# Six instead of fourteen whole-float32 products, k loaded by two heads, and a new written-out order of steps

## The chip, the cores and the metric

The kernel runs on one core of one Trainium2 chip. The metric is the device time of one execution in microseconds (us), the median of three runs. TensorE (PE in the profile) multiplies, VectorE (DVE) and ScalarE (ACT) do the elementwise work, GpSimd (POOL) and SyncE (SP) mostly start transfers (DMA). The engines run side by side, and each takes its own instructions strictly in the order in which the program lists them.

## The reference

Everything is float32. For 8 images with 8 heads, 576 positions and 64 features per head:

```python
q_s = softmax(q over features);  k_s = softmax(k over positions)
kv  = einsum('bhsd,bhse->bhde', k_s, v)          # 64 x 64 per head
x   = einsum('bhsd,bhde->bhse', q_s, kv)         # rows of 512
h   = x @ w_in                                   # 512 -> 2048
out = (h * cos(h)) @ w_out                       # 2048 -> 512
```

## The kernel before

Images 0, 1, 2 go through the two big products one after the other in *units*: unit (b, f) takes image b's 512 main rows and the f-th of 16 slices of 128 columns of `w_in`. Its first product (`unit1`) gives h in a PSUM bank, `gated` forms h·cos(h) with four instructions that alternate between ScalarE (`turns`, L1144), VectorE (`rest`, L1148), ScalarE (`cos`, L1154) and VectorE (`gate`, L1159), and the second product (`unit2`) multiplies by a slice of `w_out` into four accumulators. Units 0 to 7 are image 0 with f = 0 to 7, units 8 to 15 image 1 with f = 0 to 7; then come image 0 and image 1 with f = 8 to 15, and image 2. There are two banks for h, so the first product of unit u waits for the gate of unit u-2. Images 3 to 7 and the rows left over from all images follow as three pairs with a seven-product scheme (`block`, L1491).

A product in units is done in one of two ways. *Split*: each operand is held as a high part that TensorE's fast float32 form takes exactly, and a low rest; three of these matmuls replace one (L1119, L1204). Making the parts costs a copy on ScalarE (`hi`, `late_hi`) and a subtraction on VectorE (`lo`, `late_lo`) for each operand: for a slice of weights (`split` in `convert`), for x (`late`), for the gated h (`split_g`). *Whole*: the operands stay plain float32, and one matmul takes longer (L1111, L1197). `XP` is the number of units of image 0 whose first product is whole (8), `F2` the number of units whose second product is whole (6). For these the weights wait in a spare place (`room`) and their parts are made later. Weights need two ScalarE and two VectorE instructions (`bias`, `bits`, `shift`, `sign`) before any use.

Attention of each image (`k_exps`, `k_steps`, `q_steps`, `x_steps`) runs in between: q and k by two groups of four heads, maximum and exponent on VectorE, GpSimd and ScalarE, kv and x on TensorE. At the start TensorE also multiplies zeros (`fill`, `warm_up`).

`Plan` collects all this as numbered steps, each with an engine and an assumed duration: 0.69 us for a VectorE instruction on 128x512, 0.60 to 0.66 for one on ScalarE. The list `ORDER` holds the step numbers, and the program is emitted in that order; the list alone sets the order of each engine's instructions and of SP's transfers. An instruction waits for its operands by semaphore, and everything behind it on its engine waits too.

A load of k is a step of `load_k` on SP: one transfer of 512 KB (four heads) and one of 64 KB (left-over rows). The first v load (`load_v`, image 0, first group) is one of 512 KB and one of 64 KB; all other v loads are of two heads.

Of the kernel before, what the change touches and what calls it, by code (L numbers as in the profile page):

```python
# [27 lines left out]
    XP=8,  # L28
# [3 lines left out]
    F2=6,  # L32
# [15 lines left out]
    bus=dict(k=1.13, q=1.24, v=1.12, i=1.6, o=1.4),  # L48
# [323 lines left out]
def linear_attention_then_cos_gated_mlp(  # L372
# [247 lines left out]
    def load_k(b, a, place, due, eng="SP"):  # L620
# [9 lines left out]
        def load_main():  # L630
            t, q_of = T["k4", b, a], QUEUE[eng]
            q_of.dma_start(
                t[:, :, 0:CM, :], src[:, 0:NM, :].rearrange("h (p c) d -> p h c d", c=CM)
            )
# [5 lines left out]
        def load():  # L640
            load_main()
            load_left()
# [1111 lines left out]
```

## Time and profile before

| | |
|---|---|
| median of 3 runs | 860.26 us (857.47 to 862.21) |
| the profiled execution's own time | 860.02 us |
| its span, first to last instruction | 858.2 us |
| granted TensorE clock, mean | 0.995 of full speed |
| busy: TensorE, weight load, VectorE, ScalarE, GpSimd | 98%, 76%, 71%, 63%, 11% |
| HBM | 175 GB/s over the span |

Busy shares are of the whole span. The page also cuts the span into 40 slices and follows one chain of releases back from the last instruction; other views group instructions by line, list who waited for whom, or give the busy time of every engine in a chosen stretch. A matmul on whole float32 leaves two records and so counts twice there ("x8" for four matmuls).

### The profile page before, as it was taken

To read this page: it belongs to the slowest core of one execution; us is meant where nothing else is said; L and a number is where in the kernel's file an instruction comes from. 1 tells how busy PE (TensorE), PEld (TensorE's weight loads), DVE (VectorE), ACT (ScalarE), POOL (GpSimd) and SP (SyncE) were. 2 spreads that over 40 slices of the span, in tenths; PEclk is the share of its full clock that TensorE was granted. 3 is DMA by queue.
4 is the path that set the end of the run, shared out by engine and by line. 5 is a ranking of instruction groups with operands and counts; after the bars stand their busy time and mean duration, and the time that the engine had idled before them with its cause. 6 is when DMAs were issued, how large, how long until landed. Compare 5 with 4: busy or idle time off the path is not lost.

```text
span 858.2 us, 12494 instructions
## 1 busy us (share of the span) xinstructions
PE 838.4 (98%) x4292; PEld 656.1 (76%) x4292; DVE 609.0 (71%) x989; ACT 536.9 (63%) x1065; POOL 92.8 (11%) x149
## 2 busy tenths in 40 slices
PE   5999999999999999999999999999999999999997
PEld 5754788777777777777777888887788888888886
DVE  6798889988888878786776867855458646454543
ACT  5789899869678465765754855445446544453441
POOL 1100100110100101112112011111100211021000
PEclk9899999999999999999999999999999999999999
DMA  9972497634888895786776685665633736162213
GB/s 227 291 222 92 154 249 205 205 96 130 225 274 264 255 352 155 192 239 179 206 226 178 186 202 133 195 178 142 194 90 106 210 101 179 49 197 62 62 39 109
DMA packets 162495, 151.31 MB, mean 176 GB/s; under 512 B 66432, under 2 KB 128640, under 8 KB 162432
## 3 DMA queue, kind: packets, MB, share of 16 engines
q1 hardware_dynamic: 142080, 105.94, 42.7%
q0 software_dynamic: 19968, 44.05, 18.1%
q8 instruction: 34, 0.56, 0.3%
q10 hardware_dynamic: 384, 0.52, 0.2%
q14 instruction: 29, 0.24, 0.1%
HBM read 107.74 MB, written 42.73 MB: 175 GB/s over the span
## 4 chain that ended last, share of the span: by engine, by line
PE 75%; DMA 10%; SPq 5%; issue 5%; ACT 2%; DVE 2%; POOL 0%; DVEq 0%; ACTq 0%; POOLq 0%
PE acc L1204 35%; PE z L1491 13%; PE a L1491 10%; PE h L1119 7%; PE h L1111 3%; PE acc L1197 2%; DMA out_dram<-o 2%; PE x L966 2%; PE kv L813 2%; DMA k<-in_k_dram 1%; SPq L944 1%; DMA q_left<-qb 1%; DMA v<-in_v_dram 1%; SPq L666 1%; DMA s<-w_own 1%
## 5 line engine op out<-in xcount | busy, mean ns | idle before, releaser
L1491 PE MATMUL z<-xs,s 128*128 128x512 f32 x576 | 146.7, 391 | 1.0 <-DMA s<-w_sums 0.4
L1491 PEld LDWEIGHTS z<-xs,s 128*128 128x128 f32 x576 | 107.4, 188 | 26.3 <-issue 2.1
L1119 PE MATMUL h<-x,w_i 128*128 128x512 f32 x480 | 115.8, 392 | 1.5 <-DVE kt L1159 1.5
L1491 PE MATMUL a<-xs,s 128*128 128x512 f32 x432 | 109.9, 390 | 0.3 <-DVE kt_('s', 0, 1, 3)_3626 L1159 0.3
L1119 PEld LDWEIGHTS h<-x,w_i 128*128 128x128 f32 x480 | 89.2, 188 | 23.0 <-DVE kt L1159 2.8
L1204 PE MATMUL acc<-w_o,ghi 128*128 128x512 f32 x336 | 105.2, 394 | 1.0 <-DVE o L1246 0.9
L1491 PEld LDWEIGHTS a<-xs,s 128*128 128x128 f32 x432 | 80.9, 188 | 18.4 <-DVE glo_('s', 1, 2, 0)_5905 L1179 0.8
L1204 PEld LDWEIGHTS acc<-w_o,ghi 128*128 128x128 f32 x336 | 62.2, 188 | 18.2 <-issue 2.7
L1204 PE MATMUL acc<-w_o,glo 128*128 128x512 f32 x168 | 65.5, 390 | 0.0
L1512 DVE TENSOR_TENSOR c<-a,c 128x512 f32<-128x512 f32 x48 | 33.0, 688 | 35.6 <-PE a L1491 35.6
L1505 ACT COPY c<-z 128x512 f32<-128x512 f32 x48 | 28.1, 586 | 46.2 <-PE z L1491 38.2
L1465 POOL DMA_DIRECT2D s<-w_sums x48 | 30.2, 631 | 199.2 <-PE a L1491 130.9
L1465 POOL DMA_DIRECT2D s<-w_own x48 | 30.5, 636 | 195.0 <-PE z L1491 96.6
L1512 DVE TENSOR_TENSOR c<-z,c 128x512 f32<-128x512 f32 x24 | 16.6, 690 | 43.3 <-PE z L1491 32.7
L870 ACT ACTIVATE q<-q,qm 128x64 f32<-128x64 f32 x126 | 42.0, 337 | 1.8 <-DVE qm L857 1.8
L1144 ACT ACTIVATE kt<-h 128x512 int32<-128x512 f32 x48 | 28.5, 595 | 22.9 <-PE h L1119 20.2
L1148 DVE SCALAR_TENSOR_TENSOR kt<-kt,h 128x512 f32<-128x512 int32 x48 | 32.7, 680 | 10.7 <-ACT kt L1144 10.7
L762 POOL PARTITION_ALL_REDUCE m<-m x32 | 27.4, 901 | 110.1 <-DVE m L756 107.2
L1154 ACT ACTIVATE stash<-stash 128x512 f32<-128x512 f32 x48 | 30.1, 630 | 12.4 <-DVE stash L1148 12.4
L1204 PEld LDWEIGHTS acc<-w_o,glo 128*128 128x128 f32 x168 | 31.5, 188 | 6.7
L1154 ACT ACTIVATE kt<-kt 128x512 f32<-128x512 f32 x48 | 30.5, 635 | 9.8 <-DVE kt L1148 9.5
L1159 DVE TENSOR_TENSOR kt<-kt,h 128x512 f32<-128x512 f32 x42 | 28.4, 677 | 8.0 <-ACT kt L1154 8.0
(887 smaller groups left out, 1795.0 us busy)
## 6 DMA issues: line engine op xcount, KB each, us to landing
s<-w_sums POOLq DMA_DIRECT2D x48, 512.0 KB, 5.1
s<-w_own POOLq DMA_DIRECT2D x24, 512.0 KB, 4.8
q<-in_q_dram SPq DMA_DIRECT2D x32, 256.0 KB, 3.6
k<-in_k_dram SPq DMA_DIRECT2D x16, 512.0 KB, 5.2
raw_i<-in_moe_w_in_dram SPq DMA_DIRECT2D x16, 512.0 KB, 6.3
raw_o<-in_moe_w_out_dram SPq DMA_DIRECT2D x16, 512.0 KB, 6.2
v_sb<-in_v_dram SPq DMA_DIRECT2D x30, 256.0 KB, 4.7
q_rows<-qb SPq DMA_DIRECT2D x96, 64.0 KB, 2.7
```

The lines of the kernel that those rows point to most:

```text
L762: nc.gpsimd.partition_all_reduce(T["m", b, a][:, hs].rearrange("p h d -> p (h d)"), T["m1", b, a][:, hs].rearrange("p h d -> p (h d)"), P, ...
L870: nc.scalar.activation(t[:, r], t[:, r], AF.Exp, bias=m[:, r : r + 1], accum_out=o[:, r : r + 1])
L1119: nc.tensor.matmul(o, a, x, start=(c == 0 and n == 0), stop=(c == KC - 1 and n == 2))
L1144: nc.scalar.activation(t.bitcast(I32), src(), AF.Identity, bias=0.25, scale=1.0 / TWO_PI)
L1148: nc.vector.scalar_tensor_tensor(t, t.bitcast(I32), -TWO_PI, src(), op0=ALU.mult, op1=ALU.add)
L1154: nc.scalar.activation(t, t, AF.Sin, bias=0.5 * math.pi)
L1159: nc.vector.tensor_mul(o, t, src())
L1204: nc.tensor.matmul(T["acc", j], a[:, js], w, start=(first and n == 0), stop=(last and n == 2))
L1465: nc.gpsimd.dma_start(t, src)
L1491: nc.tensor.matmul(o, a, x, start=(first and c == 0 and m == 0), stop=(c == 1 and m == 2), skip_group_check=not first,)
L1505: "ACT", 0.6, lambda: nc.scalar.copy(cell(place), T["z" + to, k, n]),
L1512: lambda: nc.vector.tensor_add(cell(place), T["z" + to, k, n], cell(place)),
```

## The change

`XP` becomes 4 and `F2` 2: the first products of units 4 to 7 and the second products of units 2 to 5 are split. Their weights no longer wait in a room but pass at once through the two places `wc`; image 0's x is needed in parts from unit 4 on, and the gated h of units 2 to 5 is split too. The 512 KB transfer of k becomes two of 256 KB, by two heads each, in every load; the first load of v becomes two of 256 KB, by halves of its columns. `ORDER` is another list, 3050 numbers instead of 3036.

```diff
-    XP=8,
+    XP=4,
-    F2=6,
+    F2=2,
...
-        def load_main():
-            t, q_of = T["k4", b, a], QUEUE[eng]
+        def load_main(i):
+            t, q_of, hs = T["k4", b, a], QUEUE[eng], slice(2 * i, 2 * i + 2)
             q_of.dma_start(
-                t[:, :, 0:CM, :], src[:, 0:NM, :].rearrange("h (p c) d -> p h c d", c=CM)
+                t[:, hs, 0:CM, :], src[hs, 0:NM, :].rearrange("h (p c) d -> p h c d", c=CM)
             )
...
         def load():
-            load_main()
+            load_main(0)
+            load_main(1)
             load_left()
...
-            plan.load(CFG["bus"]["k"] * 2, load, writes=places, due=due, parts=2, eng=eng)
+            plan.load(CFG["bus"]["k"] * 2, load, writes=places, due=due, parts=3, eng=eng)
...
-        def get_main(src, main):
+        def get_main(src, main, x=slice(0, 2)):
+            n = main.shape[1] // 2
             QUEUE[eng].dma_start(
-                main[:, :, 1 : WV - 1],
-                src[:, 0:NM, :].rearrange("h (p x c) d -> p x h (c d)", x=2, c=2),
+                main[:, x.start * n : x.stop * n, 1 : WV - 1],
+                src[:, 0:NM, :].rearrange("h (p x c) d -> p x h (c d)", x=2, c=2)[:, x],
             )
...
-            plan.load(CFG["bus"]["v"] * 1.7, load_main, writes=place, due=due, eng=eng)
+            for x in range(2):
+                plan.load(CFG["bus"]["v"] * 0.85, lambda x=x: load_main(x), writes=[place[x]], due=due, eng=eng)
```

The two lists can be read against the steps. Up to the first product of unit 11 (image 1, f = 3; the last VectorE step that it needs is the gate of unit 9, for the bank) they hold:

| listed before it | old list | new list |
|---|---|---|
| TensorE steps | 62, of them 11 whole products of units | 62, of them 3 |
| VectorE steps, to the gate of unit 9 | 126 | 136: five low parts of g, four low parts of weights and one low part of x more |
| ScalarE steps, to the `cos` of unit 9 | 116, with 8 changes between exponent and sine | 117, with 6 |

From this product on both lists hold the same TensorE work. SP's first loads stand in this order, image 0 where no other is named. Old: q (first group), k (first), k (second), a slice of `w_in`, v left-over, q (second), a slice of `w_out`, v (first, 512 KB), a slice of `w_in`, v (second). New: q (first), k (first, in halves), v left-over, k (second, in halves), a slice of `w_out`, one half of v (first), q (second), the other half of v, two heads of v (second), a slice of `w_in`. At the end of the kernel both lists hold the same steps; the four last output blocks are taken in another order.

## Rows read from the trace of the kernel before

**Rows 1.** The page's busy line: engine, busy us, share of span, instructions.

```profile
PE 838.4 (98%) x4292; PEld 656.1 (76%) x4292; DVE 609.0 (71%) x989; ACT 536.9 (63%) x1065; POOL 92.8 (11%) x149
```

**Rows 2.** Busy by stretch: from:to, then us, each engine, clock, DMA share, GB/s.

```profile
0.00:25.00 25.00, 16.06 (x108) 14.36 (x109) 15.48 (x37) 13.21 (x46) 4.46 (x12) 0.91 0.92 228
25.00:110.00 85.00, 85.00 (x483) 49.71 (x482) 75.28 (x121) 74.94 (x124) 7.38 (x11) 0.99 0.61 185
110.00:200.00 90.00, 90.00 (x505) 72.08 (x505) 80.84 (x124) 76.91 (x191) 4.91 (x6) 1.00 0.62 180
200.00:450.00 250.00, 244.64 (x1334) 190.53 (x1331) 199.14 (x336) 171.07 (x358) 30.56 (x48) 1.00 0.79 230
450.00:800.00 350.00, 349.88 (x1644) 285.97 (x1643) 213.23 (x337) 180.19 (x318) 44.72 (x71) 1.00 0.53 150
800.00:858.00 58.00, 52.85 (x234) 43.44 (x232) 25.06 (x38) 20.55 (x35) 0.72 (x1) 0.99 0.21 59
```

**Rows 3.** Waits of TensorE, whole span: total us, times, longest.

```profile
PE kv L813 <- DMA v<-in_v_dram: 4.4, 1, 4.4
PE h L1119 <- DVE kt L1159: 1.5, 3, 0.8
```

**Rows 4.** Chain in order of time, 40 to 110: start, us, what.

```profile
46.21 3.43 PE h L1111 x8
...
64.04 3.43 PE acc L1197 x8
...
97.67 2.73 PE acc L1204 x12
100.40 2.72 PE h L1119 x12
```

**Rows 5.** Timeline around unit 11's first product: start, us, engine, line, tiles.

```profile
102.90 0.69 DVE L1159 TENSOR_TENSOR kt<-kt,h 128x512 f32<-128x512 f32 x1 [0.88 <-ACT kt L1154]
...
106.41 0.96 PE L1119 MATMUL h<-x,w_i 128*128 128x512 f32 x3
```

**Rows 6.** Timeline of VectorE, one stretch without a wait.

```profile
52.19 0.68 DVE L589 SCALAR_TENSOR_TENSOR room_o<-raw_o 128x512 int32<-128x512 int32 x1
52.79 0.68 DVE L1148 SCALAR_TENSOR_TENSOR kt<-kt,h 128x512 f32<-128x512 int32 x1
53.39 0.69 DVE L578 SCALAR_TENSOR_TENSOR raw_i<-raw_i 128x512 int32<-128x512 int32 x1
```

**Rows 7.** Waits of VectorE between 25 and 110.

```profile
DVE kt L1148 <- ACT kt L1144: 3.1, 4, 1.5
DVE r L821 <- PE kv L813: 1.5, 2, 0.9
DVE kt L1159 <- ACT kt L1154: 1.3, 2, 0.9
DVE qs L876 <- ACT q L865: 1.3, 1, 1.3
DVE g L1159 <- ACT kt L1154: 0.5, 1, 0.5
DVE glo L1179 <- ACT ghi L1175: 0.5, 1, 0.5
```

**Rows 8.** Waits of VectorE between 0 and 25.

```profile
DVE r L821 <- PE kv L813: 2.1, 1, 2.1
```

**Rows 9.** Timeline of SP: the first v load is issued.

```profile
13.74 0.60 SPq L697 DMA_DIRECT2D v<-in_v_dram  x1
```

**Rows 10.** Transfers by line: issuer, count, KB each, median us to landing.

```profile
q<-in_q_dram SPq DMA_DIRECT2D x32, 256.0 KB, 3.6
k<-in_k_dram SPq DMA_DIRECT2D x16, 512.0 KB, 5.2
```

**Rows 11.** Waits of SP's queue, whole span, those of the q loads.

```profile
SPq L661 <- PE kv L813: 67.0, 11, 15.3
```

**Rows 12.** Timeline of ScalarE: one change between exponent and sine.

```profile
54.16 1.28 ACT L1154 ACT_TABLE_LOAD   x1
```

More of the change, by code (lines that the diff above doesn't have):

```diff
@@ L645, in load_k @@
         if b:
-            plan.load(CFG["bus"]["k"] * 2, load, writes=places, due=due, parts=2, eng=eng)
+            plan.load(CFG["bus"]["k"] * 2, load, writes=places, due=due, parts=3, eng=eng)
         else:
-            plan.load(CFG["bus"]["k"] * 1.7, load_main, writes=places[:2], due=due, eng=eng)
+            for i in range(2):
+                plan.load(CFG["bus"]["k"] * 0.85, lambda i=i: load_main(i), writes=[places[i]], due=due, eng=eng)
             plan.load(CFG["bus"]["k"] * 0.3, load_left, writes=places[2:], due=due, eng=eng)
@@ L712, in load_v, with load_main @@
             src = v[b, 4 * a : 4 * a + 4]
-            def load_main():
+            def load_main(x):
                 main, last = v_parts(T["v4", b, a], 4)
-                get_main(src, main)
+                get_main(src, main, slice(x, x + 1))
                 for i in range(2):
```

315 rows, old and new, of the table ORDER are left out of this document.

## Prediction

> **What bounds the kernel now.** I start with the page's busy line: TensorE is busy 98% of the span, VectorE 71%, ScalarE 63% [rows 1]. An average over stages doesn't say which engine sets the pace in which stage, so next comes the table of stretches [rows 2]. From 25 to 200 us TensorE is busy without a hole (85.00 of 85, 90.00 of 90). From 200 to 450 it has 5.4 us of holes, from 450 to 800 0.1, and the last 5.1 us are the tail after the last matmul. In the first 25 us it has 8.9 us of holes, and the list of its waits names the largest single one: kv waits 4.4 us for the first v [rows 3]. So the end of the kernel is TensorE's work plus the start, plus about 5 us of later holes. But between 25 and 110 us VectorE is busy 75.28 of 85 and ScalarE 74.94: TensorE leads there by a small margin, and that is the stretch in which the change takes work from TensorE and gives some to VectorE.
>
> How small the margin is shows at one place, the first product of unit 11. It starts at 106.41; the last VectorE step that it needs, the gate of unit 9, runs from 102.90 to 103.59 [rows 5]. TensorE is 2.8 us behind VectorE there. From this product on both lists hold the same TensorE work, so, later holes aside, **the change is worth what this start moves**.
>
> **The change part by part.**
>
> *Eight products are split.* A whole product of a unit takes 3.43 us on the chain, a split one 2.72, for first and second products alike [rows 4]. Eight times 0.71 is 5.7 us less TensorE work, all of it before unit 11 (11 whole products listed before it become 3). On TensorE alone the start would go from 106.4 to 100.7.
>
> *What the parts cost VectorE.* Up to the gate of unit 9 the new list holds 136 VectorE steps for 126, and all ten more are subtractions on 128x512. Such an instruction is 0.68 to 0.69 us long, but without a wait the next starts 0.60 after it (52.19, 52.79, 53.39) [rows 6]. Ten times 0.60 is 6.0 us more. With the waits of before, the gate of unit 9 would end at 103.6 + 6.0 = 109.6, and TensorE would have to wait for it: 3.2 us *later* than 106.4. So the saving is not there unless VectorE loses less time, and the question is which of its waits go.
>
> *The first v.* In the new list of SP one slice of `w_in` and one of `w_out`, 512 KB each, no longer stand ahead of the first v, and one slice of `w_out` does; 512 KB less is 2.3 us at the 228 GB/s of that stretch [rows 2]. TensorE's 4.4 us wait [rows 3] shrinks by as much, and VectorE's 2.1 us wait for the same kv [rows 8] goes. I take 2.1 off; bounds: none (another operand late instead) to 2.3. The old issue at 13.74 [rows 9] moves past q and k of the second group, which the new list puts partly behind the halves of v.
>
> *VectorE's other waits between 25 and 110.* VectorE is idle 9.7 us there [rows 2]; 8.2 of that are the six waits of the view, 5.4 of them for ScalarE's results in the gate chain and its split [rows 7]. The plan puts a VectorE step at 0.69 us and the chip lets it take 0.60: over 126 steps VectorE runs about 11 us ahead of what the old list expects and stands for 8 of them, because ScalarE and TensorE give their results no earlier. In the new list ten more instructions stand where it waited. ScalarE helps: one step more, but six changes of its table for eight, each 1.28 us [rows 12], so 2.6 us less. I take 5.9 of the 8.2 us as filled; bounds: nothing to all. Then the gate of unit 9 ends at 109.6 - 2.1 - 5.9 = 101.6, and with it TensorE starts 4.8 us earlier than 106.4. With nothing filled and no gain at the start it is +3.2; with both full, 109.6 - 2.3 - 8.2 = 99.1, which is 7.3 us earlier, and TensorE's own limit (100.7 less up to 2.3) allows it.
>
> *k in two halves.* The bytes are the same. A 512 KB load lands in 5.2 us, one of 256 KB in 3.6 [rows 10]. Bounds for the first k: 1.6 us gained (both halves land like one q) to 2.0 lost (one after the other, 7.2). I take zero: the second half is issued 0.60 us behind the first, the length of an issue [rows 9], and both move together. A loss would be covered, since kv waits for v 4.4 us longer than for k; without that cover it moves kv by up to 2.0. The Trainium skill, "DMA: Bandwidth & Descriptors", section "Rules for kernel authors", speaks against this edit: it asks for at least 1 MiB in a transfer and to join small ones. The rows agree that the smaller load moves fewer bytes per us (71 KB for 98). By the rule the first k would be 2.0 us late and the time 2.0 higher if v's wait did not cover it. Later k loads: 14 times one more issue of 0.60 on SP, ahead of the next q load; SP stands 67 us waiting at q loads for kv [rows 11], so nothing; if that cover is gone, 0.6 per load.
>
> *Places for the newly split weights.* They now use the two places `wc` at once instead of a room, so the `sign` of a third slice waits for the `lo` of the first. Both are VectorE steps in list order, so it costs VectorE nothing; ScalarE's `hi` between them can make it wait about one 0.6 us instruction, and that lies within the bounds above.
>
> *The rest of the list.* Between 200 and 450 TensorE's holes are 5.4 us [rows 2]; of its waits behind the start the largest is 1.5 us, three times for a gate [rows 3]. A new list can close them (-5.4) or open as many again (+5.4). Unit and pair work is the same, so I take zero. The tail of 5.1 us stays.
>
> **Sum.** Profiled execution 860.0 (span 858.2 and 1.8 around it) - 4.8 = 855.2. That execution stands 0.24 below the median of the three runs, so 855.4.
>
> **Rivals.**
> 1. *VectorE becomes the bound and keeps its waits.* The ten subtractions add 6.0 us to an engine that is 2.8 us ahead, the order around them brings its own waits, and v's place in the queue gives nothing because `w_in` comes later (it now stands behind v and half of the second v). Price +3.2: 863.4, slower than before. It decides where VectorE's idle time up to the gate of unit 9 falls by less than 3.2 us. For it: 75.28 of 85 busy before anything is added. Against it: ScalarE has two table changes fewer.
> 2. *The list fills everything.* Unit 11 starts 7.3 us earlier and half of the holes from 200 to 450 close (-2.7): 850.2. For it: TensorE has no hole from 25 to 200 even now. Against it: no waits at all on VectorE is the very end of the bounds.
> 3. *The gain is given back later.* Unit 11 starts 4.8 us earlier, and the new list runs into a transfer between 200 and 450, where the DMA share is 0.79 [rows 2], and doubles the holes (+5.4): 860.9, no change. For it: the highest steady DMA share. Against it: the bytes are the same.
> 4. *VectorE instructions don't overlap in the new order.* If each of the 136 took its 0.69 us and not 0.60, the gate of unit 9 would come 12 us later than 101.6, at 113.8, 7.4 us behind the old start: 867.6. Against it: the spacing of 0.60 between different lines and tiles [rows 6]. The Trainium skill, "VectorE: DVE Perf Modes", section "The DRAIN you can't avoid", has the next operation start only when the pipe of the one before is empty, and excepts one that is not held. By the rule without its exception every step would take its full length; the trace shows starts 0.08 us ahead of the end, so the chance is small.
>
> **How the numbers follow.** Two measurements of this kernel within about 0.5% (4.3 us) can't be told apart. Chances: the forecast (855.4, itself give or take 2.5) 0.52, rival 1 0.15, rival 2 0.15, rival 3 0.16, rival 4 0.02. Faster by over 0.5% means under 856.0: 0.31 of the forecast's 0.52, all of rival 2 and a little of rival 3, 0.48. Slower means over 864.6: about a third of rival 1, a little of rival 3 and rival 4, 0.10. The rest, 0.42, is no change. The range goes from rival 2's side, 849, to rival 1, 863.5.
>
> **What would show it.** The groups of whole products halve or better (4 first products for 8, 2 second ones for 6), and TensorE's busy time is some 5.7 us lower. The gate of unit 9 ending near 101.6 and unit 11's first product right behind it: TensorE would then show waits for VectorE between 40 and 105, which it has none of now. The first kv starting near 19 instead of 21.1. VectorE busy nearly all of 25 to 105. Wrong would be: VectorE's idle time between 25 and 110 still at 8 us or more (rival 1), the first kv no earlier, holes between 200 and 450 well over 5.4 us (rival 3), or unit 11 starting by 99 (rival 2).

## The result, and the profile after

The changed kernel takes 863.89 us (median of 20 runs, 856.06 to 870.41), the kernel before, run beside it, 857.08 (20 runs, 853.69 to 862.21). The ratio is 1.0069, 95% interval 1.005 to 1.0089: slower by 6.8 us, where 855.4 was forecast. The profiled execution took 864.76 us, its span is 863.0, its mean granted clock 0.989 (before 0.995).

First the page's busy line of the changed kernel, to be read beside [rows 1], then its busy time by stretch, in the columns of [rows 2]:

```profile
PE 839.9 (97%) x4324; PEld 665.7 (77%) x4324; DVE 612.6 (71%) x993; ACT 536.7 (62%) x1067; POOL 96.9 (11%) x149
```

```profile
0.00:25.00 25.00, 17.98 (x106) 15.63 (x107) 16.83 (x39) 13.30 (x45) 5.69 (x12) 0.87 0.91 236
25.00:110.00 85.00, 84.46 (x536) 58.59 (x534) 82.64 (x131) 76.57 (x129) 10.47 (x11) 1.00 0.71 208
110.00:200.00 90.00, 89.51 (x511) 70.84 (x510) 74.56 (x116) 77.92 (x189) 4.69 (x6) 1.00 0.57 172
200.00:450.00 250.00, 243.06 (x1295) 191.62 (x1294) 195.91 (x330) 164.73 (x350) 29.29 (x46) 0.98 0.76 218
450.00:800.00 350.00, 347.45 (x1632) 281.85 (x1631) 214.87 (x336) 180.89 (x318) 45.72 (x73) 1.00 0.53 151
...
300.00:310.00 10.00, 8.13 (x28) 4.47 (x27) 4.19 (x8) 6.08 (x9) 0.00 (x0) 0.83 0.63 199
...
330.00:340.00 10.00, 7.36 (x33) 5.76 (x31) 8.31 (x16) 6.45 (x10) 1.61 (x3) 0.97 0.88 240
340.00:350.00 10.00, 9.89 (x65) 8.37 (x66) 6.61 (x11) 5.18 (x8) 1.64 (x3) 0.69 0.70 183
```

From 25 to 110 us VectorE is now busy 82.64 of 85, before 75.28. TensorE's busy time did not fall: 839.9 us, before 838.4. Eight split products should take 5.7 off; against that stand 1.9 us more in the first 25 us and some 5 us in which the lower clock made the same work longer. TensorE's holes from 200 to 450 are 6.9 us (before 5.4), from 450 to 800 they are 2.6 (0.1), and in three slices between 300 and 350 the granted clock is below 1.00, where it was 1.00 before. At half the clock for part of a slice the loss is one minus the mean: 1.7 + 0.3 + 3.1 = 5.1 us. The 0.3 falls into the hole that ends at 340.11 and delays nothing, so 4.8 us count.

The list of TensorE's waits (total us, times, longest) says for what, and the timeline (start, us, and in brackets the idle time before) where. The rows that answer [rows 5] come first:

```profile
PE x L971 <- DMA qf<-q_rows: 3.5, 3, 1.9
PE kv L818 <- DMA v_sb<-in_v_dram: 2.7, 1, 2.7
...
PE kv L818 <- DMA v<-in_v_dram: 1.9, 1, 1.9
PE kv L818 <- ACT k L780: 1.7, 1, 1.7
PE acc L1209 <- ACT o L1254: 1.3, 1, 1.3
```

```profile
101.42 0.68 DVE L1164 TENSOR_TENSOR kt<-kt,h 128x512 f32<-128x512 f32 x1
...
102.16 3.02 PE L1124 MATMUL h<-x,w_i 128*128 128x512 f32 x12 [0.23 <-DVE kt L1164]
...
305.09 1.83 PE L971 MATMUL x<-qf,kvw 64*64 64x512 f32 x6 [1.87 <-DMA qf<-q_rows]
...
327.58 1.39 PE L818 MATMUL kv<-v_sb,k 128*64 128x66 f32 x40
...
340.11 2.44 PE L818 MATMUL kv<-v_sb,k 128*64 128x66 f32 x40 [2.75 <-DMA v_sb<-in_v_dram]
342.47 2.93 PE L1496 MATMUL z<-xs,s 128*128 128x512 f32 x6
...
351.19 1.52 PE L1496 MATMUL z<-xs,s 128*128 128x512 f32 x6
```

Up to unit 11 this execution, set beside that of [rows 5], went nearly as forecast: the gate of unit 9 ends at 102.10 and unit 11's first product starts at 102.16, 4.25 us earlier than 106.41. (Other profiles of the old head, further down, show that 106.41 was unusually late.) Behind it, at 305, x waits 1.9 us for `qf`, at 340 kv waits 2.75 us for v, and what follows runs slowly: a kv of the same size takes 2.44 us for 1.39, six products of 128x512 take 2.93 for 1.52. The two profiled spans differ by 4.8 us. The terms: -4.25 to unit 11, +0.5 holes from 110 to 200, +1.6 from 200 to 450, +2.4 from 450 to 800, +4.8 clock, together +5.0.

### The profile page after: what moved, and what is told of

Same layout as the page of the kernel before. It is cut to its first block, busy times and chain, and to the rows that moved or that the text cites. A ratio compares the mean times of both kernels' runs of the same rounds, so it can differ in the third digit from the quotient of the medians.

```text
span 863.0 us, 12599 instructions
## 1 busy us (share of the span) xinstructions
PE 839.9 (97%) x4324; PEld 665.7 (77%) x4324; DVE 612.6 (71%) x993; ACT 536.7 (62%) x1067; POOL 96.9 (11%) x149
## 4 chain that ended last, share of the span: by engine, by line
PE 67%; ACT 6%; DMA 5%; issue 4%; DVE 3%; SPq 3%; POOL 1%; DVEq 0%; ACTq 0%; POOLq 0%
PE acc L1209 32%; PE z L1496 14%; PE a L1496 10%; PE h L1124 7%; ACT q L875 2%; PE kv L818 1%; PE x L971 1%; DMA v_sb<-in_v_dram 1%; DMA qf<-q_rows 1%; DMA s<-w_own 1%; DMA q<-in_q_dram 1%; ACT L1159 1%; DMA s<-w_sums 1%; ACT kt L1159 1%; POOL m L767 1%
## 5 line engine op out<-in xcount | busy, mean ns | idle before, releaser
L1124 PE MATMUL h<-x,w_i 128*128 128x512 f32 x528 | 129.0, 395 | 0.7 <-DVE kt L1164 0.7
L1124 PEld LDWEIGHTS h<-x,w_i 128*128 128x128 f32 x528 | 98.7, 189 | 28.0 <-DVE kt L1164 2.8
L1209 PE MATMUL acc<-w_o,ghi 128*128 128x512 f32 x368 | 114.9, 393 | 0.0
L1209 PEld LDWEIGHTS acc<-w_o,ghi 128*128 128x128 f32 x368 | 68.2, 188 | 16.7 <-issue 2.4
L1209 PE MATMUL acc<-w_o,glo 128*128 128x512 f32 x184 | 71.8, 390 | 0.2 <-DVE glo L1184 0.2
L767 POOL PARTITION_ALL_REDUCE m<-m x32 | 31.6, 1026 | 183.6 <-DVE m L761 139.9
L1209 PEld LDWEIGHTS acc<-w_o,glo 128*128 128x128 f32 x184 | 34.5, 188 | 7.9 <-DVE glo L1184 0.7
L1164 DVE TENSOR_TENSOR kt<-kt,h 128x512 f32<-128x512 f32 x46 | 31.1, 680 | 4.3 <-ACT kt L1159 3.9
```

Of the source, the lines that this page charges most:

```text
L767: nc.gpsimd.partition_all_reduce(T["m", b, a][:, hs].rearrange("p h d -> p (h d)"), T["m1", b, a][:, hs].rearrange("p h d -> p (h d)"), P, ...
L1124: nc.tensor.matmul(o, a, x, start=(c == 0 and n == 0), stop=(c == KC - 1 and n == 2))
L1164: nc.vector.tensor_mul(o, t, src())
L1209: nc.tensor.matmul(T["acc", j], a[:, js], w, start=(first and n == 0), stop=(last and n == 2))
```

## The experiments

Theory T at the outset: behind unit 11 the new order loses some 9 us. Rivals: R1, halves of k keep SP too busy; R2, whoever comes 4 us early runs into late transfers, in any order. A trace shows one execution, which need not be a typical one. Medians stand beside those of the kernel before in the same session (856.8 to 858.0).

**Is it the halves of k?**

```diff
 e3_k_whole: the changed kernel, k of images 1 to 7 in one transfer again
-            load_main(0)
-            load_main(1)
+            q_of.dma_start(t[:, :, 0:CM, :], src[:, 0:NM, :]...)
 e4_k_halves: the kernel before, k of images 1 to 7 in halves (the reverse edit)
```

> The changed kernel with the four-head k transfer of 512 KB in one piece again for images 1 to 7 (image 0 keeps its halves); list unchanged. T: no change against the changed kernel, 863 to 864. R1: the loss behind unit 11 goes, 854 to 856. R2: no change, 864.

> The kernel before with only the k transfer of images 1 to 7 in two halves of two heads; list unchanged. T: no change against the kernel before, 857. R1: some 5 to 9 us slower, 862 to 866. R2: no change.

Measured: e3 864.33 us, ratio to before 1.007 (1.0048 to 1.0093), with x waiting up to 3.6 us for `qf` and kv 3.7 for v in its trace (an execution of 868.31); e4 857.47, ratio 1.001 (0.9993 to 1.0028). R1 falls from both sides.

**Where does the new order lose?** Five kernels follow one list up to a point and the other list from there (e2 with the steps of the kernel before, the others with those of the changed one).

```diff
 ORDER = [
-    (one list)
+    e1_new_head:  new list to unit 11 (110 us),  then old
+    e2_new_tail:  old list to unit 11,           then new
+    e7_head_182:  new list to 182 us,            then old
+    e13_head_285: new list to 285 us,            then old
+    e8_head_385:  new list to 385 us,            then old
 ]
```

> The changed kernel (splits, halves and all) with its new list only up to the first product of unit 11, and behind it every step in the order of the old list. Theory T (the new order of the steps behind unit 11 loses some 9 us, the head gains 4): unit 11 starts near 102 as in the changed kernel, and the time is some 4 us under the kernel before, about 853, or 0.995 of it. Rival R1 (k in halves slows SP and its transfers): the halves are still there, so 860 to 864. Rival R2 (coming 4 us early is itself what runs into transfers that land too late, in any order): holes of TensorE behind 200 us grow by about 4 us, and the time is that of the kernel before, 857.

> The kernel before (fourteen whole products, whole k loads) with its old list up to the first product of unit 11 and behind it every step in the order of the new list. T: the head's 4 us are not gained and the tail's 9 are lost, about 866, or 1.010 of the kernel before. R1: no halves, so as the kernel before, 857. R2: not early, so as the kernel before, 857.

> The changed kernel's steps in the new order up to about 182 us (unit 17 or so), from there in the order of the old list, at a place where the two lists have done nearly the same work. Theory T: the 4.2 us of the head are kept, the waits for qf at 305 and v at 340 and the low clock behind them are not there, as in the old list; about 853. Rival R2 (whoever is 4 us early runs into late transfers, in any order): holes from 200 to 450 of 9 us or more, 857 or more. A seam that costs by itself shows as a wait right at 182.

> The changed kernel's steps in the new order up to about 385 us, then in the order of the old list. Theory T: the holes and the low clock from 300 to 350 stay as in the changed kernel, the 2.5 us of holes from 450 to 800 go: about 861. Rival: if the loss sits behind 385, about 855.

> The changed kernel's steps in the new order up to about 285 us, then the order of the old list; between e7_head_182 (857.4) and e8_head_385 (864.7). Theory D (three places where transfers are used too soon: 240, 305 and 340) puts only the first of them into the new part: about 858 to 859, holes from 300 to 350 of 1 us or less and a clock of 1.00 there. Rival: the loss is spread evenly, 861; or it sits at the front, 864.

Measured: e1 862.29 (1.0061, 1.0041 to 1.008), e2 877.06 (1.0227, 1.0203 to 1.0252), e7 857.36 (0.9994, 0.9977 to 1.0011), e13 864.84 (1.0097, 1.0059 to 1.0135), e8 864.69 (1.0068, 1.0038 to 1.0097). None met the time that its theory gave: 853 for e1 and e7, 866 for e2, 858 to 859 for e13 and 861 for e8. At 110 us the two lists have done too different work, and the seam costs by itself: a wait of 4.5 us for a gate in e1, of 9.1 for the row copies in e2. So these two don't settle it, but e2, whose head is the old one and not early, shows the tail's waits all the same (`qf` 2.4, v 2.6), which R2 doesn't allow. At 182 and 385 the lists stand close: e7 waits 1.4 us for a gate at 184, e8 at most 0.5 us for anything behind 385. The stretch of 300 to 350 in e7 and in e8:

```profile
300.00:350.00 50.00, 49.24 (x297) 39.78 (x296) 40.50 (x62) 32.99 (x55) 6.43 (x10) 1.00 0.77 236
```

```profile
300.00:350.00 50.00, 43.96 (x254) 33.55 (x253) 35.70 (x58) 26.62 (x45) 5.96 (x8) 0.90 0.74 219
```

The new order between 182 and 385 us makes the difference of 7.3 us between them: 0.8 against 6.0 us of holes, clock 1.00 against 0.90. R2 falls: both have the same new head (unit 11 at 102.78 and 102.94), and only e8 meets late transfers. e13 settles nothing more: its seam costs 2.7 us of waiting for a gate at 293, and 3.1 us of waiting for `qf` at 303 stand right behind it. Its rival, that the loss sits ahead of 285, is not excluded. And in e8 TensorE's holes from 450 to 800 are 0.4 us (changed kernel 2.6), yet its time is that of the changed kernel: those holes are not the loss.

**Are they late transfers?** Two kernels bring SP's transfers forward.

```diff
 e5_v_first: SP, image 5
-    q (first group), v, v (second group)
+    v, v (second group), q (first group)
 e6_three_moved: the same, and for images 3 and 4
-    image 4: v, q_rows, qf, ql, x_main, k, qf
+    image 4: q_rows, qf, ql, qf, v, x_main, k
-    image 3: x_main, w_sums, q_rows, w_sums, o, ql, qf, qf
+    image 3: q_rows, x_main, w_sums, ql, qf, qf, w_sums, o
```

> The changed kernel with one edit: on SP the two v loads of image 5's second group stand ahead of the q load that now stands ahead of them (nothing else moves). In the changed kernel kv waited 2.7 us for them at 340.1 and the granted clock fell to 0.69 from 340 to 350 (3.1 us). Theory T (single late transfers behind unit 11 and the clock that their holes take away are the loss): the v loads are issued at about 329 instead of 331.9, the wait is gone, the clock of 340 to 350 is 1.00 again, and the time falls by 2.7 + 3.1 to about 858. Rival G (the gain is given back whatever is mended, since the next wait takes over): another wait within the following 20 us takes the 2.7 us, time 862 or more. Rival C (the clock falls for another reason than the hole): the wait goes, the clock of 340 to 350 stays at about 0.7, time about 861.

> The changed kernel with the order of SP mended at three places, no other engine touched: v of image 5's second group ahead of the q load; for image 4 the last q_rows transfer ahead of the v loads and its qf ahead of the k load; for image 3 the last q_rows transfer ahead of one x_main and one w_sums transfer and its qf ahead of a w_sums and an o one. Theory T: the waits of x for qf at 240 (1.5 us) and 305 (1.9) and of kv for v at 340 (2.7) go, 6.1 us, and with them most of the 5 us of lowered clock between 300 and 350; time 863.9 - 6.1 - 4 to 5, about 853, below both kernels. Rival G: holes from 200 to 450 stay at 5 us or more, time 860 or more.

Measured: e5 869.96 (1.0129, 1.0098 to 1.016), e6 865.81 (1.0097, 1.0072 to 1.0122). Theory T in that form is wrong, rival G right: neither edit brought a transfer forward without another coming late. Kv no longer waits for v, but q now lands later, VectorE stands at q's maximum, and TensorE at what VectorE has queued behind it. First e5, then e6:

```profile
340.32 1.35 DVE L856 TENSOR_REDUCE qm<-q 128x18 f32<-128x1152 f32 x1 [5.73 <-DMA q<-in_q_dram]
...
342.93 0.81 PE L1490 MATMUL z<-xs,s 128*128 128x512 f32 x2 [3.78 <-DVE xs L1403]
```

```profile
341.22 1.35 DVE L856 TENSOR_REDUCE qm<-q 128x18 f32<-128x1152 f32 x1 [6.43 <-DMA q<-in_q_dram]
...
343.83 1.22 PE L1490 MATMUL z<-xs,s 128*128 128x512 f32 x2 [4.48 <-DVE xs L1403]
```

The trace of e6 is a typical execution (865.65 us). That of e5 is not: it took 862.94, the other five 868.07 to 870.92, and no trace shows where those five lose the rest.

That gave theory D. Both q and v of image 5 go into places that kv of its first group frees. In the old kernel's timeline that kv starts at 329.19 and kv of the second group at 350.11, 20.9 us later:

```profile
329.19 1.39 PE L813 MATMUL kv<-v_sb,k 128*64 128x66 f32 x40
...
350.11 1.39 PE L813 MATMUL kv<-v_sb,k 128*64 128x66 f32 x40
```

In the new one it is 327.58, and the next is due at 340.11 - 2.75 = 337.36, 9.8 us later. SP needs 5.7 us to issue the eight transfers of q and v, and v was there 5.4 us after the last issue. The first and the last of the eight in the changed kernel:

```profile
329.05 0.65 SPq L664 DMA_DIRECT2D q<-in_q_dram  x1
...
333.90 0.81 SPq L707 DMA_DIRECT2D v_sb<-in_v_dram  x1
```

So the list, not the queue, puts the use too close behind the release.

**Is the distance the cause?** e11 draws the same cluster together in the old list; e9 and e10 move the users back in the new one.

```diff
 e11_before_near: the old list, image 5
-    q, ... 7 us of TensorE work ..., q_max, ... k_exp, v, v, kv (second group)
+    q, v, v, q_max, ... k_exp, ... kv (second group, 3 us earlier)
 e9_later_340: the new list, image 5
-    q, v, v, q_max, kv (second group), q_sub, q_exp, ...
+    q, v, v, ... some 10 us of TensorE work ..., q_max, kv (second group), q_sub, q_exp, ...
 e10_later_all: e9, and for images 3 and 4
-    k_max, x (second half), products of the next units
+    products of the next units, x (second half), k_max
```

> The kernel before with the same cluster of image 5 drawn together: VectorE's maximum of q stands right behind SP's q load as in the new list (it stood 7 us of TensorE work behind it), both v loads behind q at once, kv of the second group 3 us earlier. Nothing else is changed. Theory D: VectorE stands 3 to 5 us at q, what it splits for TensorE comes late, TensorE gets a hole of 2 to 4 us near 335 to 340 and the clock falls there: 860 to 863. Rival: the old list has room enough, 857.

> The changed kernel's list with one cluster moved: kv of image 5's second group on TensorE (it waited at 340.1) and VectorE's and ScalarE's q steps of its first group stand some 10 us of TensorE work later; no transfer is moved ahead. Putting v ahead of q (e5) only let q come late, and VectorE stood 5.7 us at q's maximum. Theory D (distance): in the old list 19.9 us of TensorE work lie between kv of image 5's first group, which frees the places, and kv of the second; in the new one 9.6, less than SP's issues and the landings need, so that whatever is loaded last is late. With the distance restored the holes of 330 to 350 (2.7 us) go and the clock of 340 to 350 stays 1.00 (3.1 us): about 858. Rival G: the hole moves on to another transfer in the next 30 us, 862 or more.

> As e9_later_340, and in the same way x of image 4's second half (it waited 1.9 us at 305) with the maximum of k that VectorE stood 3.3 us at, and x of image 3's second half (1.7 us at 240) with its k maximum, stand behind one or two products of units that stood behind them. Theory D: the 6.1 us of waits for transfers from 200 to 450 go, the clock from 300 to 350 is 1.00, and the head's 4 us come through: about 853. Rival G: holes of 5 us or more from 200 to 450 all the same, 860 or more. Between: 856, if only the waits go and the clock falls elsewhere.

Measured: e11 863.71 (1.0068, 1.0045 to 1.0091), 6.9 us more than before from one cluster of one image. VectorE's and TensorE's timeline of e11, and the slice of 330 to 340 in e11 and in the kernel before:

```profile
331.22 1.35 DVE L851 TENSOR_REDUCE qm<-q 128x18 f32<-128x1152 f32 x1 [4.45 <-DMA q<-in_q_dram]
...
333.23 1.22 PE L1485 MATMUL a<-xs,s 128*128 128x512 f32 x2 [3.27 <-DVE xs L1398]
...
335.83 2.93 PE L1485 MATMUL z<-xs,s 128*128 128x512 f32 x6 [1.38 <-DVE kt L1153]
```

```profile
330.00:340.00 10.00, 5.39 (x12) 3.83 (x13) 7.63 (x11) 2.33 (x5) 1.98 (x3) 0.66 0.53 130
...
330.00:340.00 10.00, 9.60 (x59) 7.70 (x56) 8.64 (x15) 4.74 (x9) 4.10 (x6) 1.00 0.78 202
```

The chain can be followed in four rows: q lands late, VectorE stands 4.45 us, its splits come 3.27 and 1.38 us late to TensorE, and TensorE's clock falls (2.93 us for six products that take 1.52).

The way back works in part at most: e9 862.04 (1.005, 1.0031 to 1.0069), e10 860.83 (1.0037, 1.0016 to 1.0058), 3 us less than the changed kernel, at the edge of what the runs can tell. Theory D's times (858 and 853) are missed, and rival G's (862 and 860 or more) are met. In e9's trace the hole at 340 and the low clock behind it are gone (TensorE busy 10.0 of 10 from 310 to 350), but ahead of the moved cluster, at 302, x waits 3.7 us for `qf`. In e10's profile the waits for `qf` are gone, that for v is 0.7, and the clock is 1.00, but TensorE's holes are not:

```profile
300.00:350.00 50.00, 45.60 (x278) 34.80 (x277) 38.69 (x62) 32.60 (x54) 6.99 (x11) 1.00 0.83 239
...
320.00:330.00 10.00, 9.46 (x73) 7.40 (x74) 10.00 (x18) 7.68 (x13) 1.29 (x2) 1.00 1.02 302
```

VectorE is busy 10.0 of 10 from 320 to 330, and TensorE waits in pieces of 0.4 to 1.4 us, most of them for VectorE's splits and gates. This execution took 858.10, 2.7 less than e10's median. So of the 7.3 us about 3 are given back by moving three clusters, if the difference is real; the other 4 lie in the rest of that order, and no run here takes them apart.

**What does the lower clock cost?** e12 and e14 fill the two holes with products whose results the products behind them overwrite; no step moves.

```diff
 e12_filled (e14_filled_less: range(3) and range(2))
+            if (b, a) == (5, 1):      # ahead of kv
+                for _ in range(6):
+                    nc.tensor.matmul(x[0:D, 0:TB], t[:, 0, 0, :], kk[:, 0:TB], start=True, stop=True)
...
+            if (b, a) == (4, 1):      # ahead of x
+                for _ in range(4):
+                    nc.tensor.matmul(banks[0][0:D, 0:NM], T["kv", b, 2][0:D], T["qf", b, 2][0:D], ...)
```

> The changed kernel with products without use where TensorE waited for a transfer: 6 of 64x512 in plain float32 (some 2.6 us) just ahead of kv of image 5's second group, which waited 2.75 us at 340, and 4 (some 1.7 us) ahead of x of image 4's second half, which waited 1.9 us at 305. Their results are overwritten by the products behind them. No step moves and no transfer comes sooner. Theory K (the hole lowers the clock, and the lower clock costs as much again): kv and x start when they did, TensorE was not idle before, the granted clock of 300 to 310 and of 340 to 350 is 1.00 instead of 0.83 and 0.69, and the time falls by 4 to 5 us to about 859.5. Rival L (the clock falls there whatever TensorE does, or the clock's loss is covered): the clock stays at 0.7 to 0.85 in one of the two, or the time stays at 863 to 865.

> As e12_filled with half of the idle products: there the clock of 300 to 350 was 1.00, but the fill ran 0.9 and 1.8 us past the landings of qf and v (x at 305.9, kv at 341.0 to 341.9), which took back half of what the clock gave. Here 3 products (2.4 us) ahead of kv and 2 (1.8 us) ahead of x end before the transfers land. Theory K (a lower clock behind a hole is a loss of its own): clock 1.00 or near it from 300 to 350, x and kv where they stood in the changed kernel, time 2 to 4 us lower, 860 to 862. Rival L (the clock's loss is covered by VectorE, which stands late there anyway): the waits for VectorE behind 345 grow by as much and the time stays at 864.

Measured: e12 864.07 (1.0089, 1.0057 to 1.0121), e14 862.27 (1.0064, 1.0041 to 1.0086). In e12 the fill ran past the landings and took back what the clock gave. In e14 it ends before them. Its timeline from the fill (`kv<-k`) on, and its slices:

```profile
337.46 2.79 PE L811 MATMUL kv<-k 128*64 128x512 f32 x6
341.29 1.39 PE L822 MATMUL kv<-v_sb,k 128*64 128x66 f32 x40 [1.04 <-DMA v_sb<-in_v_dram]
342.61 1.65 PE L1505 MATMUL z<-xs,s 128*128 128x512 f32 x6
...
349.54 1.52 PE L1505 MATMUL z<-xs,s 128*128 128x512 f32 x6
```

```profile
300.00:310.00 10.00, 9.47 (x37) 5.38 (x37) 5.11 (x10) 6.61 (x10) 0.00 (x0) 1.00 0.68 203
...
340.00:350.00 10.00, 8.96 (x74) 7.37 (x74) 7.69 (x14) 5.92 (x9) 1.92 (x3) 1.00 0.69 186
```

The clock is 1.00 in both slices, so the holes cause its fall. From kv to the z product in the last row it is 8.25 us, in the changed kernel 351.19 - 340.11 = 11.08: 2.8 us from the clock behind one hole of 2.75 us. In the whole time 1.6 us of it are seen, within the spread of the runs, and e12's time is that of rival L. In e14's traced execution x waits 2.4 us for `qf` at 240 (1.5 in the changed kernel) and the clock of 240 to 250 is 0.83, which takes back 2.6 us. So the cost of the lower clock is shown row by row, not in the time of the kernel.

**How much did the earlier v give?**

```diff
 e15_v0_early: the old list, SP's first loads
-    w_in, v left-over, q (second), w_out, v (first)
+    w_in, v left-over, v (first), q (second), w_out
```

> The kernel before with one part of the change alone: on SP the first group's v stands ahead of q of the second group and of a slice of w_out; nothing else. In the old head TensorE sets the pace (eleven whole products), and its rest of kv waited 2.3 to 4.4 us for this v. Theory H (the old head is bound by TensorE and moves by what v moves; the new head is bound by VectorE and so keeps little of it): kv's rest starts near 17 instead of 19.3 to 21.1, unit 11's first product at 101 to 102 instead of 103.2 to 106.4, no loss behind it, time 855 to 855.5. Rival: q of the second group and the w_out slice come late instead, unit 11 as before, 857.

Measured: 858.01 (0.9997, 0.9977 to 1.0017). kv no longer waits for v, and the next step waits instead (timeline, then the list of TensorE's waits):

```profile
16.50 1.39 PE L807 MATMUL kv<-v,k 128*64 128x66 f32 x40 [0.42 <-ACT k L769]
...
104.29 3.02 PE L1113 MATMUL h<-x,w_i 128*128 128x512 f32 x12
```

```profile
PE qt L908 <- DVE q L879: 3.0, 1, 3.0
```

The rival holds: q of the second group came late in v's place, and unit 11 starts no earlier than in other profiles with the old head. Those are the second thing to see here: unit 11's first product starts at 104.08 in e2, 103.78 in e4 and 103.19 in e11. In e4:

```profile
19.74 2.22 PE L818 MATMUL kv<-v,k 128*64 128x65 f32 x36 [2.97 <-DMA v<-in_v_dram]
...
103.78 3.02 PE L1124 MATMUL h<-x,w_i 128*128 128x512 f32 x12
```

In the profile that the forecast was read from, v happened to land late (21.09), unit 11 began at 106.41, and the execution's 860.02 us stand 2.9 above the median of before's 20 runs. With the new head it begins between 101.43 and 103.47, 102.6 in the mean of twelve profiles. The old head's mean over e2, e4 and e11 is 103.7. The head's gain is then 1.1 us, not 4.25 (1.8 if the profile of [rows 5] is counted in), and what is lost behind it 6.8 + 1.1 = 7.9 us, of which e8 and e7 put 7.3 between 182 and 385. That agrees with e7, which has the new head and the old middle and is 0.6 us faster than before, which is no difference that can be measured.

VectorE's gate of unit 9 was early in those three executions too (e2, e4, e11, in this order; 102.90 in [rows 5]):

```profile
100.57 0.69 DVE L1153 TENSOR_TENSOR kt<-kt,h 128x512 f32<-128x512 f32 x1 [0.89 <-ACT kt L1148]
...
100.27 0.69 DVE L1164 TENSOR_TENSOR kt<-kt,h 128x512 f32<-128x512 f32 x1 [0.89 <-ACT kt L1159]
...
99.67 0.69 DVE L1153 TENSOR_TENSOR kt<-kt,h 128x512 f32<-128x512 f32 x1 [0.89 <-ACT kt L1148]
```

It ended there at 100.4 to 101.3, in the mean at 100.9, and in the twelve profiles with the new head at 101.4 to 103.4, in the mean at 102.5. So the change made VectorE 1.6 us later, not 2.0 earlier. Unit 11 starts 2.8 us behind that gate in all five profiles with the old head and 0.06 us behind it in all twelve with the new: the new head goes at VectorE's pace, and its gain is what VectorE's delay leaves of the 2.8 us.

No version that beats both kernels came out; e7_head_182 equals the kernel before.

## Why the prediction was wrong

Point by point, by its own steps:

- *Eight products are split*: right for the products; the sign named for it, 5.7 us less busy time of TensorE, did not show (1.5 more, see above). The groups of whole products between 25 and 110 (busy us, mean ns) halve and better, from 64 and 48 records to

```profile
L1116 PE MATMUL h<-x_whole,room_i 128*128 128x512 f32 x32 | 14.9, 602 | 0.0
...
L1202 PE MATMUL acc<-room_o,g 128*128 128x512 f32 x16 | 7.5, 599 | 0.0
```

- *What the parts cost VectorE* and *VectorE's other waits*: right in what they say of 25 to 110. VectorE is idle 2.4 us there instead of 9.7 (7.8 to 8.7 in e2, e4, e11), and 2.0 of that are waits, where 8.2 - 5.9 = 2.3 were forecast. That the gate of unit 9 then ended at 102.10, so near the forecast 101.6, is luck: 101.6 was counted from the late 103.6 of [rows 5].
- *The first v*: **this term failed.** Kv's rest starts at 18.23, 2.9 us earlier than in [rows 3]'s execution and 1.0 to 1.9 earlier than in e11, e4 and e2. But of the 2.1 us for VectorE little was there to be gained: its wait for that kv was 1.2, 0.6 and 0.5 us in e2, e4 and e11, and in the changed kernel it waits longer for q instead (4.6 us in the first 25, for 3.7 to 4.3). So the lower bound, "another operand late instead", comes nearest to what the rows show. From the mean of those three the prediction's own steps give 100.9 + 6.0 - 2.1 - 5.9 = 98.9 for the gate, again 4.8 us ahead of the start at 103.7; measured is 102.5, and the start gained 1.1. Some 1.5 us of that gap no run explains. (Also, k of the second group stands ahead of v in both lists; only q was passed.)
- *k in two halves*: right at zero for images 1 to 7 (e4: ratio 1.001), with 4.4 us to landing in the changed kernel for each half and 5.2 for the whole before. The halves of image 0 were not tried alone; the first kv, which waits for them, starts at 16.01 (16.37 before). The Trainium skill, "DMA: Bandwidth & Descriptors", section "Rules for kernel authors", asks for at least 1 MiB in a transfer where bandwidth is the goal; e4 shows no price for going the other way here.
- *The rest of the list, taken as zero*: **this step failed, and it is the larger one.** It rested on unit and pair work being the same in both lists, with bounds of 5.4 us either way. The work was the same, the distance between the release of a place and the use of what is loaded into it was not. The new order between 182 and 385 costs 7.3 us (e8 against e7). That short distances make such a loss is shown by e11 (6.9 us from one cluster); that they are all of the 7.3 is not, since e10 gives back about 3.
- *Rival 3* named the mechanism (the gain is given back at a transfer between 200 and 450) and was 3 us short of the time: it let the holes double and gave them no clock. In the profile the holes of that stretch grew by 1.6 us and those behind it by 2.4, and 4.8 us came from the clock, which the prediction had nowhere as a price.
- *Rivals 1, 2 and 4* fell: VectorE kept few waits, unit 11 did not start by 99, and VectorE's instructions start 0.60 us apart as before. Rival 1's time, 863.4, is near the measured one by chance: it was right that VectorE sets the pace and that v gives little, but its loss was to lie in front of unit 11, which came earlier, not later.

In sum, a change of -4.8 us was forecast and +6.8 measured. Of the 11.6 us between them 3.7 lie in the start (-1.1 for -4.8) and 7.9 behind it.

What the profile of before could have told: image 5's two kv stood 20.9 us apart there, and the new list was known. The TensorE work between the two in the lists is 19.9 and 9.6 us by the plan's durations. Against 9.6 stand eight issues (5.5 us in the trace of before) and the landing of v (4.7, the median there), and the places are free only when the first kv has run its 1.4 us. That is an estimate of 10 us and more, which points to the place at 340 without a run, though not to the whole loss.

## What to carry to other kernels

When an order is written anew, compare for each reused place the work between its release and the next use in the old and the new list, with the issues of the whole queue and the landing in between; equal work in equal sequence on TensorE says nothing about it. The Trainium skill has the general rule ("DMA: Bandwidth & Descriptors", section "Rules for kernel authors": issue the transfer early, compute, wait for it late). e11 shows what going against it cost here: 6.9 us for one cluster. A start time from one profiled execution is one draw; take it from several profiles before a forecast of a few us is built on it.

## What the runs showed that was not expected

A hole on TensorE can cost about twice its length: behind the hole of 2.75 us at 340 the granted clock of the next 10 us was 0.69, which is part of the time at the lower level (1.2 GHz), and kv and the products behind it lost 2.8 us; with the hole filled by useless products the clock stayed at 1.00. The price does not follow the length: the other profiles show 1.7 us lost behind 3.7 us of hole (e9, at 302) and nothing behind 2.4 us (e2, at 316).

Bringing the late transfer forward on SP made the kernel slower still (e5, about 5 us more than the changed kernel when each is taken against the kernel before of its own session). In the traces of e5 and e6 VectorE then waited 5.7 and 6.4 us for the transfer that was overtaken, and TensorE 3.8 and 4.5 us for VectorE, more than the 2.75 us that were mended. e6, which holds the same edit and more, can't be told apart from the changed kernel.
